# Row maxima rounded on VectorE, output weights loaded behind them, and four smaller moves of work in a fused transformer block

## The chip, the core and the metric

The kernel runs on one core of one Trainium2 chip. The time is device microseconds of one execution, from its start to its end. Three runs of the kernel before took 1684.24, 1685.24 and 1686.47 us; their median, 1685.24 us, is the figure that a change is compared with. A further execution was taken with the hardware profiler; every row below is from it.

## The reference

A transformer block over 2048 rows of 512 numbers, in float32: layer norm with a shift and a scale, attention with 32 heads of 16, an output projection, a gated residual, then a second layer norm and a feed-forward network of 1792 with a tanh GELU.

```python
def reference(A_x, A_wqkv, A_wo, B_x, B_w1, B_b1, B_w2, B_b2, c, w_mod):
    x = A_x
    mod = (_silu(c) @ w_mod).reshape(c.shape[0], 6, 1, -1)
    sa, ca, ga, sb, cb, gb = (mod[:, i] for i in range(6))
    h = _layernorm(x, axis=-1) * (1 + ca) + sa
    x = x + ga * _A_ref(h, A_wqkv, A_wo)
    h = _layernorm(x, axis=-1) * (1 + cb) + sb
    x = x + gb * _B_ref(h, B_w1, B_b1, B_w2, B_b2)
    return x
```

`_A_ref` forms q, k and v, takes the softmax of q·k/4 over all 2048 keys for each head, multiplies it with v and projects the result with `wo`. `_B_ref` is `gelu(x @ w1 + b1) @ w2 + b2`.

## The kernel before

**Precision.** Operands of most matmuls are split into a high part (rounded to the matmul's own format) and a low part (the rest), and three products of the parts are added. That is why so many small steps "cast, then subtract" stand in the program.

**Units and half-steps.** Attention is cut into 32 *units*: a block of 512 rows (four blocks, 0 to 3) times a group of four heads. A unit has 16 *half-steps*, one for each 128 keys; there are 512 half-steps in all, numbered through. In one half-step TensorE does four score matmuls (`e`, L685), whose exponentials ScalarE takes (L692); four more score matmuls for the row maxima of a unit that comes later (`mx`, L415), which VectorE reduces (L420); up to six matmuls of *background* work on each half of the rows (`bg`, L279: projections of q, k, v at first, then output projection and feed-forward of the block before); and at its end the eight value matmuls (`pv`, L720). A row of `pv` therefore marks the end of a half-step, and the distance of two such rows is its length. When no background work is at hand, the half-step runs without it.

**Row maxima.** A softmax needs the maximum of each row before its exponentials. The 64 `mx` matmuls of a unit are spread over 16 half-steps and run `LEAD` = 80 ahead, so that a unit's last one falls into the eleventh half-step of the unit before. Their results rotate through three PSUM banks (3, 4, 5): the fourth `mx` of a half-step writes the bank that the first `mx` of the same half-step had, and must wait until VectorE has reduced that one. Where a half-step has no background work, the third `mx` goes to the background's own bank 7 instead. When the 64th reduction of a unit is recorded, `max_rows` adds four operations: VectorE takes the minimum over the key blocks (L433, values are negated) and transposes it (L435); GpSimd rounds it (L437) and forms the rest (L438). SyncE stores both to DRAM (L442) three ticks later and loads them as two extra rows of the query tile `qst` (L448) six ticks later. The first `e` of the unit needs these rows. A *tick* is one `advance()`, one exponential; a half-step has four.

**Banks.** `e` has banks 0 to 2, `mx` 3 to 5, `pv` 6, the background 7. `take(name)` hands out the next bank of a ring.

**What else the change touches.** `turn_blocks` transposes blocks of v on VectorE (L345), at most two half-steps after the projection. `attn_out` copies the finished `pv` bank to SBUF at each unit's end (L707), on VectorE. `o_prep` loads a unit's denominators, takes reciprocals on VectorE (L767), spreads them over DRAM (L771, L777) and lets GpSimd divide (`div`, L787 to L789). `wload` asks for the next weights of the background (L835): `wo`, `w1`, `w2`. After the projections of block 0, `open_ffn` opens the pools of the feed-forward, four `wload` calls ask for `wo`, and the background pauses for `OPEN` ticks. `front` runs the output projection, the second layer norm (`stat`, `factor`, `norm`) and four groups of transposes (`trans`, L918), one group per half-step. `ffn1` takes the first feed-forward product: ScalarE (L948), GpSimd (L949 to L951), ScalarE's tanh (L954) in `second`, nine ticks later, and GpSimd again (L956 to L959).

The order on each engine is the order in which the program is written out, half-step by half-step (`half_step`); each engine takes its instructions strictly in that order. The line that decides which bank the third `mx` of a half-step without background takes is in `half_step`:

```python
fs.append(mx_mm(1 - a, "bg" if free and sum(xc) == nx - 2 else "mx"))
```

Of the kernel before, what the change touches and what calls it, by code (L numbers as in the profile page):

```python
# [61 lines left out]
RUN = 6  # L62
OPEN = 12
WB = 8
# [8 lines left out]
def block_kernel(ctx: ExitStack, tc: tile.TileContext, x, wqkv, wo, w1, b1, w2, b2, c, w_mod, out):  # L73
# [276 lines left out]
    def turn_blocks(hs):  # L350
        if not blocked:
            return
        if until_hs[0] is None:
            until_hs[0] = hs + 1
        left = until_hs[0] - hs
        n = len(blocked)
        rowed_now = rowed[0] >= clock["t"] - 4
        for _ in range(n if left <= 0 else 0 if rowed_now and n <= 2 * left else -(-n // (left + 1))):
            turn_block()
# [68 lines left out]
    rows, rowed = {}, [0]  # L428

    def max_rows(u):  # L430
        rowed[0] = clock["t"]
# [4 lines left out]
        m2 = small.tile([P, 2, 32], FR, tag="m2", name="m2")  # L436
        gp.tensor_copy(m2[:, 0], mt)  # L437
        gp.tensor_tensor(m2[:, 1], mt, m2[:, 0].bitcast(F32), op=ALU.subtract)  # L438

# [264 lines left out]
    def attn_out(u, pv):  # L704
        qb, g = divmod(u, NG)
        o = kqpool.tile([P, TB], F32, tag="osb", name="osb", bufs=1)
        saw(ve.tensor_copy(o, pv))  # L707
        rowed[0] = clock["t"]
        late = u < NU - 1
# [41 lines left out]

    free_pc, busy, over = [0], [0], [False]

    def o_prep(b, k):
# [30 lines left out]

        def div():
            eng.tensor_tensor(ob, ob, rb, op=ALU.mult)  # L787
            eng.tensor_copy(pc(b, k, 0), ob)
# [4 lines left out]
        fast = 0 < b < NB - 1 and k == KC - 1  # L793
        later(11 if over[0] else 28 if b == 0 and k < KC - 1 else 9 if fast else 14, inv)

# [17 lines left out]
    for b in range(NB):  # L813
# [4 lines left out]
        if b < NB - 1:  # L818
            stream += [(b + 1, "o", k) for k in range(KC)]
    wt, used, ringed, extra = {}, set(), [], []  # L820

    def wload():

        n = len(wt)
        if n == len(stream) or "f" not in pools:
            return
# [29 lines left out]
    def front(b, x2):  # L856
# [9 lines left out]
        def norm(t):  # L866
# [4 lines left out]
            if len(xn) == 4:  # L871
                later(5, lambda: sides.extend([lambda fc=fc: trans(fc, "mx") for fc in range(KC)]))

        def stat(t):
# [9 lines left out]
            def whole():  # L884
                ve.bn_aggr(mv[:, t], st)
                factor(t)

            def calm(f):
                later(3, f) if rowed[0] > clock["t"] - 4 else f()

# [38 lines left out]
    def feed(b, x2):  # L929
# [7 lines left out]
        def ffn1(i):  # L937
            def evac(ps):
# [22 lines left out]

                later(9, second)

# [41 lines left out]
    def block0():  # L1005
# [346 lines left out]
```

## Time and profile before

| what | us |
|---|---|
| median of three runs | 1685.24 |
| profiled execution, its own time | 1683.93 |
| its span, first to last instruction | 1682.1 |
| TensorE busy | 1656.0 |
| VectorE busy | 1424.9 |
| ScalarE busy | 1211.3 |
| GpSimd busy | 716.7 |
| mean granted TensorE clock, as a share of full speed | 0.993 |

The profiled execution is 1.3 us faster than the median of the three runs and 1.8 us longer than its own span. A row of the timeline gives the start and the duration in us, the engine (PE is TensorE, PEld its weight loads, DVE VectorE, ACT ScalarE, POOL GpSimd, SPq the queue of SyncE), the line, the operation, the tile written and the tiles read, and the count of like instructions merged into the row; in brackets stands the idle time ahead of it and what ended it. A row of the groups gives the count, then the busy time, the mean duration in ns, and the idle time ahead.

### The profile page before, as it was taken

The page shows a single profiled execution, that of the slowest core. Times are in us where ns is not written, and L with a number is a line of the kernel's source. Part 1 is how long each engine was busy: PE and PEld are TensorE (multiplying, and loading weights), DVE is VectorE, ACT ScalarE, POOL GpSimd, SP SyncE. Part 2 cuts the span into 40 slices and gives each one's busy share as a digit, 9 for nine tenths or more (in the row PEclk, how much of TensorE's full clock was granted, in tenths as well). Part 3 has the DMA queues.
Part 4 walks back from the last instruction along what each step waited for, and adds up shares of the span by engine and source line. Part 5 has one row for each costly group of instructions (what it writes and reads, how often), then busy time and mean ns, then how long its engine had stood idle before and what let it go on. Part 6 is the DMA issues. An engine that isn't in the chain of part 4 may idle for free.

```text
span 1682.1 us, 32274 instructions
## 1 busy us (share of the span) xinstructions
PE 1656.0 (98%) x12079; PEld 905.8 (54%) x12079; DVE 1424.9 (85%) x2770; ACT 1211.3 (72%) x2320; POOL 716.7 (43%) x719
## 2 busy tenths in 40 slices
PE   7999999999998999999999999999999999999999
PEld 6655555555544455555555555555555555553677
DVE  7999999999898999999999899999999899990332
ACT  4367777777776788778777888778777887788131
POOL 7443544534221376216523476126434475056210
PEclk8999999999999999999999999999999999999999
DMA  8766666665546443335462554254452643252544
GB/s 289 212 196 181 222 214 207 224 175 191 152 146 200 119 113 102 78 97 142 115 170 59 152 156 106 68 141 138 106 152 56 185 128 84 64 166 72 185 152 159
DMA packets 142808, 246.97 MB, mean 147 GB/s; under 512 B 25390, under 2 KB 53052, under 8 KB 142652
## 3 DMA queue, kind: packets, MB, share of 16 engines
q1 hardware_dynamic: 140896, 243.80, 49.8%
q8 instruction: 96, 1.57, 0.4%
q10 hardware_dynamic: 1756, 1.11, 0.3%
q14 instruction: 60, 0.49, 0.1%
HBM read 184.56 MB, written 60.29 MB: 146 GB/s over the span
## 4 chain that ended last, share of the span: by engine, by line
PE 93%; DMA 3%; DVE 2%; POOL 1%; ACT 0%; SPq 0%; issue 0%; POOLq 0%; ACTq 0%; DVEq 0%
PE bg L279 40%; PE pv L720 29%; PE e L685 16%; PE mx L415 4%; PE pr L279 2%; DMA wraw<-in_A_wqkv_dram 1%; DVE mxp L420 1%; PE o L279 1%; DMA qk<-parts 0%; DVE hTlo L510 0%; PE mx L918 0%; DMA m<-m 0%; DMA wt<-wos 0%; POOL wqkv L210 0%; DMA qst<-m 0%
## 5 line engine op out<-in xcount | busy, mean ns | idle before, releaser
L420 DVE TENSOR_REDUCE mxp<-mx 128x1 f32<-128x512 f32 x2038 | 1288.1, 682 | 116.7 <-PE mx L415 102.2
L692 ACT ACTIVATE p<-e 128x512 f32<-128x512 f32 x2048 | 1072.4, 608 | 307.9 <-PE mx L415 265.6
L415 PE MATMUL mx<-kh,qst 48*128 48x512 f32 x2038 | 842.2, 424 | 0.7 <-DVE mxp L420 0.5
L685 PE MATMUL e<-qst,kh 50*128 50x512 f32 x2048 | 777.3, 423 | 10.6 <-DMA qst<-m 5.3
L685 PEld LDWEIGHTS e<-qst,kh 50*128 50x128 f32 x2048 | 342.4, 185 | 440.6 <-ACT p L692 327.2
L720 PE MATMUL pv<-p,vg 128*17 128x512 f32 x4096 | 541.1, 599 | 0.1
L415 PEld LDWEIGHTS mx<-kh,qst 48*128 48x128 f32 x2038 | 369.8, 185 | 18.8 <-DVE mxp L420 9.4
L279 PE MATMUL bg<-w,g 64*128 64x512 f32 (+1 forms) x1080 | 269.7, 389 | 0.0
L279 PEld LDWEIGHTS bg<-w,g 64*128 64x128 f32 (+1 forms) x1080 | 200.4, 186 | 30.8 <-POOL g L958 0.9
L279 PE MATMUL bg<-pchi,w 64*128 64x512 f32 x672 | 182.9, 391 | 0.0
L720 PEld LDWEIGHTS pv<-p,vg 128*17 128x17 f32 x4096 | 68.2, 95 | 170.6 <-issue 168.8
L279 PE MATMUL bg<-hThi,wqkv 64*128 64x512 f32 x560 | 153.4, 393 | 0.0
L279 PEld LDWEIGHTS bg<-pchi,w 64*128 64x128 f32 x672 | 123.9, 185 | 23.0 <-DVE tick L1135 5.1
L279 PEld LDWEIGHTS bg<-hThi,wqkv 64*128 64x128 f32 x560 | 103.9, 186 | 12.4
L956 POOL TENSOR_SCALAR s<-s 128x512 f32<-128x512 f32 x42 | 62.9, 1497 | 82.5 <-ACT s L954 81.7
L279 PE MATMUL bg<-pclo,w 64*128 64x512 f32 x336 | 91.9, 392 | 0.0
L975 POOL TENSOR_TENSOR x<-y,x 128x512 f32<-128x512 f32 x28 | 36.0, 1286 | 125.5 <-ACT y L974 125.5
L279 PE MATMUL bg<-hTlo,wqkv 64*128 64x512 f32 x280 | 76.2, 391 | 0.0
L949 POOL TENSOR_TENSOR s<-h 128x512 f32<-128x512 f32 x42 | 43.8, 1042 | 74.9 <-ACT h L948 74.9
L279 PEld LDWEIGHTS bg<-pclo,w 64*128 64x128 f32 x336 | 61.7, 185 | 14.5 <-DVE tick L1135 3.4
L279 PE MATMUL bg<-wo,pchi 64*128 64x512 f32 x192 | 60.4, 395 | 0.0
L437 POOL CAST m<-mt 128x32 fp32r<-128x32 f32 x32 | 6.8, 212 | 123.1 <-DVE mt L435 123.1
(162 smaller groups left out, 1359.3 us busy)
## 6 DMA issues: line engine op xcount, KB each, us to landing
kh<-qk SPq DMA_DIRECT2D x256, 192.0 KB
w<-w2s SPq DMA_DIRECT2D x56, 512.0 KB
w<-w1s SPq DMA_DIRECT2D x54, 512.0 KB
qk<-parts SPq DMA_DIRECT2D x32, 512.0 KB
vg<-v SPq DMA_DIRECT2D x48, 272.0 KB
qst<-qk SPq DMA_DIRECT2D x64, 192.0 KB
qk<-parts SPq DMA_DIRECT2D x32, 256.0 KB
ou<-osb SPq DMA_DIRECT2D x32, 256.0 KB
```

The costliest lines, as they stand in the source:

```text
L279: return te.matmul(ps, term[0][r], rhs, start=i == 0, stop=i == n - 1)
L415: te.matmul(ps, qst[u][r0 : r0 + KR, p, qc * P : (qc + 1) * P], kh(u, kr // 2)[r0 : r0 + KR, p, (kr % 2) * TB : (kr % 2 + 1) * TB], start= ...
L420: ins = ve.tensor_reduce(mxp[u][:, hc, kr : kr + 1], ps, axis=AX.X, op=ALU.max, negate=True)
L437: gp.tensor_copy(m2[:, 0], mt)
L685: ins = te.matmul(ps, kh(u, kc // 8)[r0 : r0 + KX, p, (kc % 8) * P : (kc % 8 + 1) * P], qst[u][r0 : r0 + KX, p], start=True, stop=True)
L692: op = ac.activation(t, ps, AF.Exp, scale=SCALE)
L720: te.matmul(pvb[32 * j : 32 * j + VW], vg[u % 2][:, n : n + VW], pt.pop(4 * s + j), start=kc == 0, stop=kc == NKC - 1)
L949: gp.tensor_tensor(s, h, h, op=ALU.mult)
L956: gp.tensor_scalar(s, s, 1.0, None, op0=ALU.add)
L975: later(4, lambda: gp.tensor_tensor(x2[t], y, x2[t], op=ALU.add))
```

## The change

```diff
-OPEN = 12
+OPEN = 14
+WAIT = 6
...
 def turn_blocks(hs):
-        rowed_now = rowed[0] >= clock["t"] - 4
+        rowed_now = rowed[0] >= clock["t"] - 4 or hs and hs % NKC == 0
         for _ in range(n if left <= 0 else 0 if rowed_now and n <= 2 * left else -(-n // (left + 1))):
...
+    def calm(f):
+        if rowed[0] > clock["t"] - 4 or cur["pv"] % NKC == NKC - 1:
+            later(2, lambda: calm(f))
+        else:
+            f()
...
 def max_rows(u):
-        gp.tensor_copy(m2[:, 0], mt)
-        gp.tensor_tensor(m2[:, 1], mt, m2[:, 0].bitcast(F32), op=ALU.subtract)
+        ve.tensor_copy(m2[:, 0], mt)
+        ve.tensor_tensor(m2[:, 1], mt, m2[:, 0].bitcast(F32), op=ALU.subtract)
...
 def attn_out(u, pv):
-        saw(ve.tensor_copy(o, pv))
-        rowed[0] = clock["t"]
+        if act["g"]:
+            saw(ve.tensor_copy(o, pv))
+            rowed[0] = clock["t"]
+        else:
+            ac.activation(o, pv, AF.Copy)
...
 def div():
+            divided[0] = clock["t"]
...
-        later(11 if over[0] else 28 if b == 0 and k < KC - 1 else 9 if fast else 14, inv)
+        later(11 if over[0] else 28 if b == 0 and k < KC - 1 else 9 if fast else 14, inv if over[0] else lambda: calm(inv))
...
 def wload():
-        if n == len(stream) or "f" not in pools:
+        if n == len(stream) or "f" not in pools or not wready:
...
-                later(5, lambda: sides.extend([lambda fc=fc: trans(fc, "mx") for fc in range(KC)]))
+                later(5, lambda: sides.extend([lambda fc=fc: trans(fc, "mx" if b or fc == KC - 1 else "bg") for fc in range(KC)]))
...
 def stat(t):
-            def calm(f):
-                later(3, f) if rowed[0] > clock["t"] - 4 else f()
...
 def ffn1(i):
-                later(9, second)
+                t0 = clock["t"]
+                later(9, lambda: later(6, second) if divided[0] > t0 - 4 else second())
...
 def block0():
         open_ffn()
+        yield from wait(WAIT)
+        wready.append(True)
         for k in range(KC):
             wload()
-        yield from wait(OPEN)
+        yield from wait(OPEN - WAIT)
```

The lines move by up to eleven: L420, L433, L435 of the kernel before are L421, L440, L442 of the changed one; its new VectorE operations are L444 and L445.

**Place one, the end of block 0's projections** (half-steps 138 to 143, unit 8). On VectorE, the row maxima of unit 9 (`mn`, `mt`, `m`), between reductions (`mxp`) of `mx` banks. Before:

```order
L420 TENSOR_REDUCE mxp<-mx 128x1 x5
L433 TENSOR_REDUCE mn_181<-mxp 128x16
L435 STREAM_TRANSPOSE mt<-mn_181 128x32
L420 TENSOR_REDUCE mxp<-mx 128x1 x2
L420 TENSOR_REDUCE mxp<-bg 128x1
```

VectorE in the changed kernel, at the same place:

```order
L421 TENSOR_REDUCE mxp<-mx 128x1 x5
L440 TENSOR_REDUCE mn_181<-mxp 128x16
L442 STREAM_TRANSPOSE mt<-mn_181 128x32
L444 CAST m_7431<-mt 128x32
L445 TENSOR_TENSOR m_7431<-mt,m_7431 128x32
L421 TENSOR_REDUCE mxp<-mx 128x1 x2
L421 TENSOR_REDUCE mxp<-bg 128x1
```

The cast and the subtraction now stand on VectorE between the transpose and the next reduction; the same two rows are gone from GpSimd. This holds for all 32 units.

SyncE at the same place: stores of projected parts (`qk`), loads of `wo`, the store of the maxima (`m`), their load into `qst`, loads of keys (`kh`) and of the first feed-forward weights (`w1s`). Before:

```order
L302 DMA qk_86<-parts 128x512
L835 DMA wo<-wos_135 128x1024
L835 DMA wo<-wos_136 128x1024
L835 DMA wo<-wos_137 128x1024
L835 DMA wo<-wos_138 128x1024
L442 DMA m_104<-m_7431 4x32x32 x2
L835 DMA w_7498<-w1s_139 128x1024
L448 DMA qst<-m_104 2x1024 x2
L387 DMA kh_194<-qk_88 48x2x512 x2
```

SyncE in the changed kernel:

```order
L303 DMA qk_86<-parts 128x512
L449 DMA m_104<-m_7431 4x32x32 x2
L455 DMA qst<-m_104 2x1024 x2
L846 DMA wo<-wos_135 128x1024
L846 DMA wo<-wos_136 128x1024
L846 DMA wo<-wos_137 128x1024
L846 DMA wo<-wos_138 128x1024
L388 DMA kh_194<-qk_88 48x2x512 x2
L846 DMA w_7566<-w1s_139 128x1024
```

The maxima and their load stand ahead of the four `wo` loads, where they stood behind them and behind one `w1s` load. The background pauses in the same half-steps as before (139 to 142, and 159 to 164).

**Place two, TensorE at the transposes of block 0** (`ident,xn`), in a half-step without background. Before, from one `pv` to the next:

```order
L685 MATMUL e<-qst,kh_193 128x512
L415 MATMUL mx<-kh_195,qst 128x512
L685 MATMUL e<-qst,kh_193 128x512
L415 MATMUL mx<-kh_195,qst 128x512
L685 MATMUL e<-qst,kh_193 128x512
L415 MATMUL bg<-kh_195,qst 128x512
L685 MATMUL e<-qst,kh_193 128x512
L415 MATMUL mx<-kh_195,qst 128x512
L918 MATMUL mx<-ident,xn 128x128 x4
L720 MATMUL pv<-p,vg_1175 17x512 x4
```

TensorE in the changed kernel, the end of the first half-step with transposes:

```order
L692 MATMUL e<-qst,kh_193 128x512
L416 MATMUL bg<-kh_195,qst 128x512
L692 MATMUL e<-qst,kh_193 128x512
L416 MATMUL mx<-kh_195,qst 128x512
L926 MATMUL bg<-ident,xn 128x128 x4
L730 MATMUL pv<-p,vg_1175 17x512 x4
```

Three of the four groups now write bank 7 (`bg`), which the third `mx` of the same half-step has just written; each group also stands one half-step later (162 to 165 instead of 161 to 164), so that the fourth falls into a half-step with background.

**Place three, GpSimd in unit 30**: two divisions (`ob`, `kh`) of the last block, and two feed-forward pieces (`s`, `h`, `g`). Before:

```order
L787 TENSOR_TENSOR ob<-ob,rb 128x512
L788 CAST kh_197<-ob 128x512
L789 TENSOR_TENSOR kh_197<-ob,kh_197 128x512
L956 TENSOR_SCALAR s<-s 128x512
L957 TENSOR_TENSOR h<-s,h 128x512
L958 CAST g<-h 128x512
L959 TENSOR_TENSOR g<-h,g 128x512
L787 TENSOR_TENSOR ob<-ob,rb 128x512
L788 CAST kh_197<-ob 128x512
L789 TENSOR_TENSOR kh_197<-ob,kh_197 128x512
L949 TENSOR_TENSOR s<-h 128x512
L950 TENSOR_SCALAR s<-s 128x512
```

GpSimd in the changed kernel:

```order
L798 TENSOR_TENSOR ob<-ob,rb 128x512
L799 CAST kh_197<-ob 128x512
L800 TENSOR_TENSOR kh_197<-ob,kh_197 128x512
L798 TENSOR_TENSOR ob<-ob,rb 128x512
L799 CAST kh_197<-ob 128x512
L800 TENSOR_TENSOR kh_197<-ob,kh_197 128x512
L964 TENSOR_SCALAR s<-s 128x512
L965 TENSOR_TENSOR h<-s,h 128x512
L966 CAST g<-h 128x512
L967 TENSOR_TENSOR g<-h,g 128x512
L957 TENSOR_TENSOR s<-h 128x512
L958 TENSOR_SCALAR s<-s 128x512
```

The second part of the first piece moved behind the second division; both still stand ahead of the second piece. On ScalarE the tanh of the first piece moved from half-step 486 to 488; the tanh of the second piece stays at the end of half-step 490. In unit 31 one more tanh moved by two half-steps.

Elsewhere: two of the 32 copies of `pv` go to ScalarE (after half-step 159 and after the last one); two reciprocals stand after a unit's end instead of ahead of it (after half-step 255 and 383); some statistics move by one to three half-steps. The transposes of v stand in the same half-steps and the same order as before: `turn_blocks` meets four waiting blocks with one half-step left, and 4 <= 2·1 is false, whatever `rowed_now` is.

More of the change, by code (lines that the diff above doesn't have):

```diff
@@ L750, in tmp @@
         return dvpool.tile([P, D], F32, tag="t", name=name, bufs=4)
-    free_pc, busy, over = [0], [0], [False]
+    free_pc, busy, over, divided = [0], [0], [False], [-99]
     def o_prep(b, k):
@@ L819, in block_kernel @@
             stream += [(b + 1, "o", k) for k in range(KC)]
-    wt, used, ringed, extra = {}, set(), [], []
+    wt, used, ringed, extra, wready = {}, set(), [], [], []
     def wload():
         n = len(wt)
-        if n == len(stream) or "f" not in pools:
+        if n == len(stream) or "f" not in pools or not wready:
             return
```

## The prediction, as it was put on record

> **What bounds the kernel now.** I read the page first, then the list of waits, then TensorE's timeline from one `pv` to the next, and last the timelines of the engines that TensorE waits for.
>
> ```profile
> PE 1656.0 (98%) x12079; PEld 905.8 (54%) x12079; DVE 1424.9 (85%) x2770; ACT 1211.3 (72%) x2320; POOL 716.7 (43%) x719
> ```
>
> TensorE is busy 98% of the span of 1682.1 us. A saving off TensorE is therefore worth only the hole in TensorE's row that it closes, and a delay elsewhere costs whatever hole it opens. So I look for holes, half-step by half-step.
>
> ```profile
> 316.96 1.05 PE L720 MATMUL pv<-p,vg 128*17 128x512 f32 x8
> ...
> 317.95 0.49 PE L415 MATMUL mx<-kh,qst 48*128 48x512 f32 x1
> ...
> 319.46 0.40 PE L415 MATMUL mx<-kh,qst 48*128 48x512 f32 x1
> 319.79 1.05 PE L720 MATMUL pv<-p,vg 128*17 128x512 f32 x8
> ```
>
> This is an ordinary half-step: 319.79 - 316.96 = 2.83 us from `pv` to `pv`. The first `mx` stands at 317.95, the fourth at 319.46, 1.51 later. It is the one in which unit 5's maxima are finished, and VectorE does this in it:
>
> ```profile
> 318.19 0.22 DVE L433 TENSOR_REDUCE mn<-mxp 128x16 f32<-128x64 f32 x1
> 318.52 0.21 DVE L435 STREAM_TRANSPOSE mt<-mn 128x32 f32<-128x32 f32 x1
> 318.65 1.84 DVE L420 TENSOR_REDUCE mxp<-mx 128x1 f32<-128x512 f32 x3
> ```
>
> The two small operations push the reduction of the first `mx` to 318.65, 0.70 after that matmul's start, and TensorE does not notice. What happens when VectorE is pushed further is seen at unit 0's end, where the copy of `pv` and two transposes of v stand ahead of the reduction:
>
> ```profile
> 148.74 1.05 PE L720 MATMUL pv<-p,vg 128*17 128x512 f32 x8
> 149.73 0.49 PE L415 MATMUL mx<-kh,qst 48*128 48x512 f32 x1
> ...
> 151.65 0.50 PE L415 MATMUL mx<-kh,qst 48*128 48x512 f32 x1
> 152.08 1.05 PE L720 MATMUL pv<-p,vg 128*17 128x512 f32 x8
> ```
>
> ```profile
> 150.92 1.87 DVE L420 TENSOR_REDUCE mxp<-mx 128x1 f32<-128x512 f32 x3
> ```
>
> The first reduction starts 1.19 after its matmul; the fourth `mx`, which needs its bank, starts at 151.65 instead of 149.73 + 1.51 = 151.24, `pv` follows it by 0.43 instead of 0.33, and the half-step takes 3.34, 0.51 too long. So with d the distance from the first `mx` to its reduction, the loss is about d - 0.69 once d is over 0.7 (0.70: nothing; 1.19: 0.51). **VectorE has no room left in the half-step of the row maxima.**
>
> **Rounding on VectorE.** It adds a cast and a subtraction of 128x32 at exactly that place. No row shows them on VectorE; their neighbours are:
>
> ```profile
> L788 DVE CAST kh<-ob 128x512 fp32r<-128x512 f32 x1 | 0.4, 426 | 0.0
> L789 DVE TENSOR_TENSOR kh<-ob,kh 128x512 fp32r<-128x512 f32 x1 | 0.7, 693 | 0.0
> L223 DVE TENSOR_TENSOR s_c<-s_c,c_c 128x4 f32<-128x4 f32 x1 | 0.2, 163 | 0.0
> L196 DVE CAST hThi<-h 128x512 fp32r<-128x512 f32 x1 | 1.1, 1082 | 0.0
> ```
>
> Between 163 ns at 4 columns and 693 at 512, the subtraction of 32 columns takes about 0.19 us. The cast is 426 at 512; with a fixed part like the subtraction's it takes about 0.17. Each operation of this chain needs the result before it, and L435 starts 0.11 after L433's end (318.41 to 318.52), while the reduction starts 0.08 ahead of L435's end. So the reduction moves by 0.11 + 0.17 + 0.11 + 0.19 = 0.58; without any waiting between them, by 0.36. I take 0.50. Then d is 0.70 + 0.50 = 1.20 and the loss 0.51 per unit, with ends of 0.37 and 0.59. It falls on 29 units: of the 31 whose successors' maxima are finished inside the loop, unit 8 has no background there and so one `mx` less in the ring, and after unit 30's there is no reduction left. 29 x 0.51 = **+14.8 us** (10.7 to 17.1), and the first unit's maxima lie on a VectorE chain at the start, +0.4. Bounds further out: nothing, if the two overlapped entirely; and, by the cast that took 1082 ns where another took 426, 2.5 times the two durations, 0.36 x 1.5 = 0.54 more, 29 x 0.54 = 16 us on top.
>
> [...]
>
> **Maxima ahead of the output weights.** The one large hole in the steady part is in half-step 143:
>
> ```profile
> PE e L685 <- DMA qst<-m: 5.3, 2, 4.8
> ```
>
> ```profile
> 502.90 0.46 SPq L302 DMA_DIRECT2D qk<-parts  x1
> 506.37 1.75 SPq L835 DMA_DIRECT2D wo<-wos  x4
> ```
>
> ```profile
> 510.11 1.05 PE L720 MATMUL pv<-p,vg 128*17 128x512 f32 x8
> 515.99 0.76 PE L685 MATMUL e<-qst,kh 50*128 50x512 f32 x1 [4.83 <-DMA qst<-m]
> ...
> 519.42 1.58 PE L720 MATMUL pv<-p,vg 128*17 128x512 f32 x8
> ```
>
> The half-step takes 519.42 - 510.11 = 9.31, 6.48 too long. The store of the maxima stood behind four `wo` loads on SyncE, which themselves waited until 506.37, and its data behind their 2 MB. TensorE stood still for 4.83 and then ran slowly (0.76 for an `e` that otherwise takes 0.49), which the next half-step also feels, by some 0.5. In the changed order the store goes out right after 503.36, the load follows before 507.5, and `e` finds its rows at 511.1. **-6.5 - 0.5 = -7.0.** What is late next is `wo`.
>
> ```profile
> 514.32 0.57 SPq L448 DMA_DIRECT2D qst<-m  x2
> ```
>
> It is asked for about 1 us later than before, near 507.4, and its first quarter is needed at 511.4; before, all four quarters and the maxima had landed by 514.32, when SyncE could go on to the load, 7.9 after the first issue. A quarter of that is 2.0, so the first should be there near 509.5 to 510.5, the second a little before its use at 512.1. I take no wait; the far end is a wait of 2 us, +2. SyncE's other issues (keys, `x`, values) move behind by the same microsecond and stand some 5 us earlier in absolute time. The second, 0.5 us wait of the two above is on maxima that GpSimd rounded late: -0.5.
>
> **Transposes in bank 7.** Before:
>
> ```profile
> 568.06 1.05 PE L720 MATMUL pv<-p,vg 128*17 128x512 f32 x8
> ...
> 572.22 1.05 PE L720 MATMUL pv<-p,vg 128*17 128x512 f32 x8
> ...
> 574.81 0.65 PE L918 MATMUL mx<-ident,xn 128*128 128x128 f32 x4
> 575.40 1.05 PE L720 MATMUL pv<-p,vg 128*17 128x512 f32 x8
> ```
>
> ```profile
> 574.98 0.68 DVE L420 TENSOR_REDUCE mxp<-bg 128x1 f32<-128x512 f32 x1
> ```
>
> The transposes start at 574.81, while VectorE reads bank 7 until 575.66. Writing that same bank they must wait for it: 0.85 to 0.9 us in each of three half-steps, +2.6; these become about 4.05 long instead of 3.18. The shift by a half-step takes the first group out of half-step 161 (4.16 long, with VectorE behind), -1.2, leaves VectorE's backlog to the next, +0.3, and puts the last group, 0.59, into a full half-step, +0.6. ScalarE's copy of `pv` there spares VectorE 0.6 at a place with slack. Sum **+2.3** (from -1, if the bank's wait were hidden, to +3.5).
>
> **The tanh.** In half-step 490 ScalarE waits in front of the second tanh:
>
> ```profile
> 1511.45 1.30 POOL L787 TENSOR_TENSOR ob<-ob,rb 128x512 f32<-128x512 f32 x1
> ...
> 1516.58 1.26 POOL L951 TENSOR_TENSOR s<-s,h 128x512 f32<-128x512 f32 x1
> ```
>
> ```profile
> 1517.88 0.63 ACT L954 ACTIVATE s<-s 128x512 f32<-128x512 f32 x1 [3.77 <-POOL s L951]
> ```
>
> GpSimd worked without a gap from 1511.45 to 1517.84, and ScalarE, with all exponentials behind that tanh, stood for 3.77. The change delays the first piece's tanh and lets the second division go ahead of its rest; but division, rest and the second piece's three operations all stay ahead of the second tanh, in another order. The same work ends no earlier, and later by whatever the second division waits for its data. I take +0.6 for that and for one tanh more in a half-step where ScalarE already has an extra evacuation (from -3.8, the whole stall, to +1.5).
>
> **The rest.**
>
> ```profile
> 841.31 0.34 DVE L767 RECIPROCAL dn<-dn 128x32 f32<-128x32 f32 x1
> ```
>
> This reciprocal, and one like it in unit 23, stood between the last reduction and the copy at a unit's end; moved out, each gives back at most its 0.34, together -0.5 with rounding up. The three ends of units 0, 2 and 4 with transposes of v, 0.5 each, stay: the order shows the transposes unmoved. The pause of 14 ticks for 12 costs nothing, since the background rests in the same half-steps; the last copy on ScalarE is as long as VectorE's.
>
> **Sum:** 14.8 + 0.4 - 7.0 - 0.5 + 2.3 + 0.6 - 0.5 = +10.1. Against the profiled execution's own 1683.9 that is 1694.0; the median of the runs shown lies 1.3 above that execution, so I put it at **1695**.
>
> **The rivals.**
>
> *The rounding is hidden* (the other side: faster). It decides at d: if the reduction still starts within 0.7 of its matmul, TensorE never waits and 14.8 goes: 1695 - 15 = 1680. For it speaks that VectorE is busy only 85% and idles later in each half-step; against it, that 0.70 is used already and that unit 0's end shows the loss at 1.19. The two operations would have to cost 0.02 together, less than a tenth of the smallest row. 8%.
>
> *The rounding is stretched* by GpSimd at work beside it, as the cast of 1082 ns was: +16, half of it more likely than all, so 1703 to 1711. For it: GpSimd is busy 43% of the span. Against: the two operations have 32 columns, and their fixed part need not stretch. 9%.
>
> *The wait moves from the maxima to `wo`*: TensorE stands at 511.4 for up to 2 us, and if it then runs slowly as it did after 515.99, for one more: 1697 to 1699. For it: the loads are asked for later and needed at the same time. Against: 4 us lie between. 10%.
>
> *The tanh or the transposes gain after all*, as a change that reorders them may mean to: -3 to -4 each at best, 1688 to 1692. Against: the orders, in which the same work stays ahead. 10%.
>
> *The change doesn't do what it says*: for the V blocks this is certain, and already in the sum at 0.
>
> **How the numbers follow.** My forecast has 63%, by its own bounds (10.7 to 17.1 for the rounding, +2 for `wo`, -3 and +1 for the transposes) 1689 to 1701. With the two rivals next to it the range must reach down to 1686 and up to 1702; outside lie the hidden rounding and most of the stretched one, some 17%. A measurement of this kernel can tell about 0.2% from no change, 3.4 us. Faster than 1681.9: 8% from the hidden rounding and 1% from several small gains together. Between 1681.9 and 1688.6: 11%, a rounding of half the price or two gains at once. Slower: 80%.
>
> **What would show it.** In the changed kernel's timeline, half-steps 16u + 11 should be 3.2 to 3.45 long with the cast and subtraction of some 0.17 and 0.19 on VectorE and d near 1.2; at 2.85 the rounding is hidden. Half-step 143 should be near 2.85 without a wait on `qst`; a wait there on `wo` is the third rival. Half-steps 162 to 164 should be near 4.05, with TensorE waiting on VectorE's `bg` reduction. The tanh in half-step 490 should still wait for L959 (L951 before) by nearly 4 us. I am wrong if the `mx` ring has slack that I don't see, or if VectorE's small operations overlap more than L433 and L435 do.

## The result, and the profile after

| | before | after |
|---|---|---|
| median, us | 1685.86 (4 runs, 1684.24 to 1686.54) | 1712.07 (4 runs, 1706.44 to 1712.49) |
| profiled execution, its own time, us | 1683.93 | 1711.76 |
| its span, us | 1682.1 | 1709.9 |
| first `pv`, last `pv`, at us | 106.3, 1561.6 | 106.6, 1589.3 |

The ratio is 1.0149, with a 95% interval from 1.0127 to 1.0172: the change made the kernel **slower by 1.5%**, 26 us, where 10 were forecast. The first row of the changed kernel's page (busy time of each engine):

```profile
PE 1669.8 (98%) x12079; PEld 905.9 (53%) x12079; DVE 1446.6 (85%) x2832; ACT 1212.7 (71%) x2322; POOL 702.9 (41%) x655
```

TensorE is busy for 13.8 us more with the same 12079 instructions, and the span is 27.8 longer. Where the rest went is found as the prediction looked for holes: all 511 intervals from one `pv` to the next are measured in both traces and subtracted, pair by pair (counted from 0, so that interval 142 is half-step 143, and the eleventh interval of unit u is half-step 16u + 11). Outside the places named here the pairs agree within some 0.04 us. Three of the places differ between profiles even where nothing was changed at them, so one pair of traces does not decide them: the start, the second wait on `qst` and the half-steps behind the tanh. They are taken up below.

| place | forecast, us | measured, us |
|---|---|---|
| row maxima: 29 eleventh half-steps, 23.1; the one behind unit 3's, 1.55; the one behind unit 8's, 0.67 | +14.8 | +25.3 |
| start, up to the first `pv` | +0.4 | +0.3 |
| maxima ahead of `wo` (half-steps 143, 144) | -7.0 | -6.5 |
| second wait on `qst` | -0.5 | -0.6 |
| rows of `x` for block 0 (half-steps 149 to 151) | 0 | +3.4 |
| transposes of block 0 | +2.3 | +3.0 |
| tanh: the half-step of the second piece's, and the four around it | +0.6 | +2.7 |
| reciprocals (0.2 each); statistics moved (0.15 at three places) | -0.5 | 0.0 |
| transposes of v | 0 | 0 |
| **sum** | **+10.1** | **+27.6** |

**The row maxima.** TensorE and then VectorE in unit 13 of the changed kernel, where GpSimd rests (start and duration in us):

```profile
750.76 1.05 PE L730 MATMUL pv<-p,vg 128*17 128x512 f32 x8
...
751.75 0.49 PE L416 MATMUL mx<-kh,qst 48*128 48x512 f32 x1
...
754.06 1.05 PE L730 MATMUL pv<-p,vg 128*17 128x512 f32 x8
```

```profile
752.07 0.22 DVE L440 TENSOR_REDUCE mn<-mxp 128x16 f32<-128x64 f32 x1
752.32 0.21 DVE L442 STREAM_TRANSPOSE mt<-mn 128x32 f32<-128x32 f32 x1
752.57 0.18 DVE L444 CAST m<-mt 128x32 fp32r<-128x32 f32 x1
752.78 0.19 DVE L445 TENSOR_TENSOR m<-mt,m 128x32 fp32r<-128x32 f32 x1
752.89 1.88 DVE L421 TENSOR_REDUCE mxp<-mx 128x1 f32<-128x512 f32 x3
```

With the first `mx` at 751.75, d is 1.14 and d - 0.69 = 0.45; the interval is 3.30, which is 0.47 over the ordinary 2.83 and 0.40 over the same half-step before (2.90). The forecast was 0.51. Now unit 4, VectorE first, then GpSimd, then TensorE at the same moment:

```profile
326.59 0.21 DVE L442 STREAM_TRANSPOSE mt<-mn 128x32 f32<-128x32 f32 x1
326.84 1.09 DVE L444 CAST m<-mt 128x32 fp32r<-128x32 f32 x1
327.96 0.53 DVE L445 TENSOR_TENSOR m<-mt,m 128x32 fp32r<-128x32 f32 x1
328.41 1.87 DVE L421 TENSOR_REDUCE mxp<-mx 128x1 f32<-128x512 f32 x3
```

```profile
326.61 1.28 POOL L316 TENSOR_TENSOR parts<-pf,parts 128x512 fp32r<-128x512 f32 x1
327.83 0.62 POOL L660 CAST wsp<-wf 128x512 fp32r<-128x512 f32 x1
```

```profile
326.08 0.49 PE L416 MATMUL mx<-kh,qst 48*128 48x512 f32 x1
...
329.14 0.50 PE L416 MATMUL mx<-kh,qst 48*128 48x512 f32 x1 [1.15 <-DVE mxp L421]
```

The cast ends at 327.93, 0.04 after GpSimd's subtraction (327.89). The next VectorE instruction ends at 328.49, 0.04 after GpSimd's cast (328.45). The small instructions are not slowed by some factor: they **stand until GpSimd's running instruction has ended**. Then d is 328.41 - 326.08 = 2.33, d - 0.69 is 1.64, and the interval was 1.65 too long: the formula held, d did not. I call this the *hold*. Over the kernel it shows in the means, which lie well above the 0.18 and 0.19 of unit 13 (groups, 32 instructions each):

```profile
L444 DVE CAST m<-mt 128x32 fp32r<-128x32 f32 x32 | 14.5, 453 | 1.1
...
L445 DVE TENSOR_TENSOR m<-mt,m 128x32 fp32r<-128x32 f32 x32 | 9.6, 301 | 1.1
...
L442 DVE STREAM_TRANSPOSE mt<-mn 128x32 f32<-128x32 f32 x32 | 6.8, 212 | 1.1
```

The transpose keeps 212. The loss is 1.2 to 2.3 us in seven of the units 0 to 7, where GpSimd prepares weights, and 1.1 in units 15 and 23, where it divides. It is 0.63 in units 9, 12, 20 and 28, where the cast is held for some 0.24, and 0.38 to 0.49 in the rest of the 29.

**Maxima ahead of `wo`, and what came behind.** SyncE's queue in the changed kernel:

```profile
516.43 1.57 SPq L449 DMA_DIRECT2D m<-m  x2
519.92 0.57 SPq L455 DMA_DIRECT2D qst<-m  x2
520.67 1.76 SPq L846 DMA_DIRECT2D wo<-wos  x4
...
528.97 0.34 SPq L720 DMA_DIRECT2D ou<-osb  x1
529.72 0.57 SPq L639 DMA_DIRECT2D vg<-v  x1
530.55 4.01 SPq L865 DMA_DIRECT2D x<-in_A_x_dram  x4
```

Half-step 143 fell from 9.31 to 3.31 us, with no wait on `qst` or `wo`. But the rows of `x` are now asked for behind the copy of `pv` and the values, and their issue alone takes 4.01. Before, they stood ahead of both:

```profile
517.66 3.29 SPq L854 DMA_DIRECT2D x<-in_A_x_dram  x4
...
522.47 0.33 SPq L710 DMA_DIRECT2D ou<-osb  x1
```

GpSimd and then VectorE in the changed kernel:

```profile
543.23 1.28 POOL L915 TENSOR_TENSOR x<-y,x 128x512 f32<-128x512 f32 x1 [27.75 <-DMA qst<-qk]
```

```profile
544.54 0.43 DVE L893 BATCH_NORM_STATS2 bsh<-x 128x6 f32<-128x256 f32 x1 [1.92 <-POOL x L915]
544.89 1.87 DVE L421 TENSOR_REDUCE mxp<-mx 128x1 f32<-128x512 f32 x3
```

The same instruction in the kernel before:

```profile
529.37 1.29 POOL L907 TENSOR_TENSOR x<-y,x 128x512 f32<-128x512 f32 x1 [26.43 <-ACT y L904]
```

ScalarE's copy of the first output group, which that instruction adds to `x`, before and after:

```profile
528.68 0.62 ACT L904 ACTIVATE y<-bg 128x512 f32<-128x512 f32 x1
```

```profile
535.82 0.62 ACT L912 ACTIVATE y<-bg 128x512 f32<-128x512 f32 x1
```

Before, the addition started 0.07 behind the copy's end; now it starts at 543.23, 6.8 behind it, and waits for a transfer. The profile names `qst` as what ended the wait, the neighbour of `x` on the queue; that it was `x` is shown by the experiment that asks for `x` sooner. VectorE waits with the statistics of `x`, the reductions that the program puts behind them wait too, and TensorE loses 3.4 in three half-steps.

**Transposes and tanh.** TensorE at the second group of transposes, and ScalarE at the tanh of the second piece:

```profile
590.55 0.66 PE L926 MATMUL bg<-ident,xn 128*128 128x128 f32 x4 [0.83 <-DVE mxp L421]
591.14 1.05 PE L730 MATMUL pv<-p,vg 128*17 128x512 f32 x8
```

```profile
1545.09 0.63 ACT L962 ACTIVATE s<-s 128x512 f32<-128x512 f32 x1 [5.75 <-POOL s L959]
```

The groups wait for the reduction of bank 7 as forecast; half-steps 162 to 164 take 4.41, 4.08 and 4.08. The tanh waits 5.75 where it waited 3.77. GpSimd shows why:

```profile
1530.31 1.28 POOL L800 TENSOR_TENSOR kh<-ob,kh 128x512 fp32r<-128x512 f32 x1
1533.67 1.29 POOL L798 TENSOR_TENSOR ob<-ob,rb 128x512 f32<-128x512 f32 x1 [2.08 <-DMA w<-w2s]
```

The second division now follows the first directly, its data are not there, and GpSimd stands idle for 2.08 us; before, the rest of the first piece filled that time. Not all of the +2.7 is this. Behind the stall TensorE's granted clock is 0.5 for 6.8 us (1544.1 to 1551.0), where in the profile of before it was 0.5 for 3.4 (1520.6 to 1524.1). So the next half-step is 0.99 longer, and it is just as much longer in seven profiles of kernels below whose tanh stands as before, with a slow clock as long as here. How much the tanh cost by itself is shown by undoing it.

### The profile page after: what moved, and what is told of

It is laid out like the page before. It is cut to its first block, busy times and chain, and to the rows that moved or that the text cites. A ratio compares the mean times of both kernels' runs of the same rounds, so it can differ in the third digit from the quotient of the medians.

```text
span 1709.9 us, 32270 instructions
## 1 busy us (share of the span) xinstructions
PE 1669.8 (98%) x12079; PEld 905.9 (53%) x12079; DVE 1446.6 (85%) x2832; ACT 1212.7 (71%) x2322; POOL 702.9 (41%) x655
## 4 chain that ended last, share of the span: by engine, by line
PE 84%; DVE 8%; DMA 4%; POOL 1%; issue 1%; SPq 1%; ACT 1%; POOLq 0%; ACTq 0%; DVEq 0%
PE bg L280 35%; PE pv L730 27%; PE e L692 15%; DVE mxp L421 5%; PE mx L416 5%; PE pr L280 1%; DMA rden<-dn 1%; DMA x<-in_A_x_dram 1%; DMA kh<-qk 1%; DVE m L444 1%; DVE bst L238 1%; DMA wm<-in_w_mod_dram 0%; PE o L280 0%; DVE m L445 0%; PE mx L926 0%
## 5 line engine op out<-in xcount | busy, mean ns | idle before, releaser
L421 DVE TENSOR_REDUCE mxp<-mx 128x1 f32<-128x512 f32 x2038 | 1288.6, 682 | 118.5 <-PE mx L416 101.9
L964 POOL TENSOR_SCALAR s<-s 128x512 f32<-128x512 f32 x42 | 62.9, 1498 | 112.5 <-ACT s L962 112.5
L280 PEld LDWEIGHTS bg<-pclo,w 64*128 64x128 f32 x336 | 61.7, 185 | 13.8 <-DVE tick L1146 4.3
L315 POOL CAST parts<-pf 128x512 fp32r<-128x512 f32 x23 | 14.1, 612 | 119.4 <-ACT pf L314 119.4
```

What stands on the lines that cost most here:

```text
L280: return te.matmul(ps, term[0][r], rhs, start=i == 0, stop=i == n - 1)
L315: gp.tensor_copy(parts[:, 0], r)
L421: ins = ve.tensor_reduce(mxp[u][:, hc, kr : kr + 1], ps, axis=AX.X, op=ALU.max, negate=True)
L964: gp.tensor_scalar(s, s, 1.0, None, op0=ALU.add)
```

## The experiments

A single profiled time is uncertain by its start: the first `pv` came between 104.3 and 108.2 us in the twelve profiles of this study, though at most two small instructions on one unit's maxima differ there. So the intervals decide, most of which repeat to some 0.02. The profile of before has one of its own: the second wait on `qst`, 0.47 in interval 110, is 0.12 in one other profile and missing in ten, also where GpSimd rounds as before. So the -0.6 there cannot be put down to the change.

### Undo the rounding; do it alone

The first kernel is the changed one with this edit; the second makes the opposite edit in the kernel before, and no other.

```diff
-        ve.tensor_copy(m2[:, 0], mt)
-        ve.tensor_tensor(m2[:, 1], mt, m2[:, 0].bitcast(F32), op=ALU.subtract)
+        gp.tensor_copy(m2[:, 0], mt)
+        gp.tensor_tensor(m2[:, 1], mt, m2[:, 0].bitcast(F32), op=ALU.subtract)
```

> The changed kernel with only the rounding of the maxima put back on GpSimd. The theory (the hold: VectorE's cast and subtraction within SBUF stand still until the GpSimd instruction that runs beside them has ended, so the rounding cost 23.1 us in the eleventh intervals of 29 units, 1.5 in the interval behind unit 3's and 0.7 behind unit 8's) says the profiled execution falls by about 25 us, from 1711.8 to 1686 or 1687, with no eleventh interval over 2.9 us. The rival (the rounding cost the 14.8 us of the prediction, and 10 us come from other parts of the change) says 1696 to 1698, with some of the long intervals left. Either way the 3.4 us at the block 0 input rows (three intervals from 148 on), the 3.0 at the transposes and the 2.7 at the tanh should stay, and the interval 142 should stay near 3.3 if the maxima ahead of the output weights are enough, or rise towards 3.8 if VectorE's quicker rounding was needed as well.

> The kernel before with nothing but the rounding of the maxima on VectorE. The hold says +25 us: 1709, with the eleventh intervals of units 0 to 7 at 1.2 to 2.3 over the ordinary 2.83 where GpSimd's TENSOR_TENSOR or CAST of the weights' preparation runs beside the cast, 0.4 to 0.5 where GpSimd rests or runs a TENSOR_SCALAR, and 1.1 to 1.2 in units 15 and 23, where it divides. The prediction's fixed price says +15: 1699, 0.51 in each of 29 units. GpSimd's program loses 64 short instructions, so the places at which it is beside the cast can move by some tenths of a us.

Measured: 1683.09 with the rounding put back, the eleventh intervals of units 0 to 29 equal to those of before within 0.03. Alone it gave 1710.07, beside 1684.93 for the kernel before on the same chip: +25.1; the intervals at the maxima sum to +24.6. So **the rounding is the whole loss**; the other parts of the change together are worth about nothing (by intervals -6.5 in half-steps 143 and 144, +1.6 at `x`, +3.0 at the transposes and +2.7 at the tanh, the latter in part the slow clock). Half-step 143 stayed at 3.33: the order on SyncE is enough there, VectorE's quicker rounding (0.18 and 0.19 us in unit 13, where GpSimd's two took 0.21 and 0.25 on average) adds nothing. In the kernel with the rounding alone unit 3 cost 2.55 + 2.28 + 0.51; the last two come with a granted TensorE clock of 0.5 from 279.2 to 286.0 us. Unit 0 lost 0.40 instead of 1.88 and unit 5 0.46 instead of 1.38: where GpSimd happens to be decides.

### The same place, instructions that are not held

```diff
         ve.transpose(mt, m)
+        ve.transpose(m, mt)
+        ve.transpose(mt, m)
```

> The kernel before with two more transposes of 128x32 behind L435 (the maxima turned back and turned again, some 0.21 us each), the rounding still on GpSimd. They stand on VectorE at the very place of the changed kernel's cast and subtraction and are about as long, but read one SBUF tile each, as the transpose that is there and is never stretched. The hold says that they cost the fixed price alone in every unit, 0.45 to 0.55 in units 0 to 7 as in the others, and 29 x 0.5 = 14.5: 1698. The rival, that whatever stands at this place of VectorE is stretched by the load of the first eight units (their memory traffic, or TensorE's), says 1.2 to 2.3 in units 0 to 7 again, and 1707 to 1709.

Measured: 1696.55, and in every unit from 0 to 29 but 8 an interval 0.42 to 0.51 longer, most 0.48, the first eight like the others. Together +13.9: the forecast's 14.8 was right for the fixed price. What is left, 25.3 - 13.9 = **11.4 us**, is the hold with the slow half-steps behind it. The split is good to about 1 us: the units of the changed kernel in which nothing is held lost 0.38 to 0.49, a little less than the transposes cost.

### A GpSimd instruction set beside the cast

```diff
         ve.tensor_reduce(m[:, :16], mxp.pop(u), axis=AX.X, op=ALU.min)
+        if u > 10:
+            d = ga_b.rearrange("p (a b) -> p a b", b=32)
+            s = m[:, None, :].to_broadcast([P, 16, 32])
+            if u % 3 == 0:
+                gp.tensor_tensor(d, s, d, op=ALU.add)
+            elif u % 3 == 1:
+                gp.tensor_scalar(d, s, 1.0, None, op0=ALU.add)
+            else:
+                gp.tensor_copy(d, s)
```

> The kernel before with the rounding of the maxima on VectorE, and beside it, for the maxima of units 11 to 31, one extra GpSimd instruction of 128x512 that starts once L434 has the maxima: a TENSOR_TENSOR (1.3 us) where the unit's number is divisible by 3, a TENSOR_SCALAR (up to 1.5 us) where it leaves 1, a COPY (0.6 us) where it leaves 2. What it writes is used by nobody. If the hold is real and belongs to the instruction, the eleventh interval of the unit before grows from 0.4 to 0.5 over 2.83 to about 1.2 to 1.6 beside the TENSOR_TENSOR (the cast takes 0.9 to 1.1 us), stays at 0.4 to 0.6 beside the TENSOR_SCALAR (cast under 0.25), and goes to 0.6 to 0.9 beside the COPY (cast 0.4 to 0.5): about 6 us in all over the kernel with the rounding alone. If the long casts of units 0 to 7 came from what those units load and store, and not from GpSimd's instruction, all three kinds leave the interval at 0.4 to 0.6.

Three units of this kernel, each VectorE's cast and GpSimd's instruction beside it:

```profile
661.70 1.13 DVE L446 CAST m<-mt 128x32 fp32r<-128x32 f32 x1
```

```profile
661.50 1.29 POOL L438 TENSOR_TENSOR ga_b<-mn,ga_b 128x512 f32<-128x512 f32 x1 [3.24 <-DVE mn L433]
```

```profile
708.51 0.45 DVE L446 CAST m<-mt 128x32 fp32r<-128x32 f32 x1
```

```profile
708.32 1.49 POOL L440 TENSOR_SCALAR ga_b<-mn 128x512 f32<-128x512 f32 x1 [6.67 <-DVE mn L433]
```

```profile
754.71 0.50 DVE L446 CAST m<-mt 128x32 fp32r<-128x32 f32 x1
```

```profile
754.56 0.61 POOL L442 COPY ga_b<-mn 128x512 f32<-128x512 f32 x1 [10.93 <-DVE mn L433]
```

Beside TENSOR_TENSOR and COPY the cast ends 0.04 after GpSimd's instruction, as expected, and the intervals are 1.4 and 0.7 longer than before (2.7 and 1.75 where a second GpSimd instruction catches the subtraction as well). Beside the TENSOR_SCALAR I was wrong: the cast takes 0.45, not under 0.25, and the intervals are 0.73 to 0.83 longer. The cast ends at 708.96, 0.64 after the TENSOR_SCALAR's start, and so does the cast beside each other TENSOR_SCALAR within 0.01; the last 0.85 us of that GpSimd record hold nobody. That also explains why the changed kernel's casts beside L964, a TENSOR_SCALAR that had started 0.45 earlier, took 0.19: 0.64 - 0.45. The kernel took 1726.56, some 16 more than with the rounding alone. I had expected about 6; the intervals of units 10 to 29 gave 12, and the slow half-steps behind units 23 and 28 another 3. I had left out the units in which two instructions are caught, and what they bring behind them.

### Which VectorE instructions are held

The kernel before, with GpSimd's TENSOR_TENSOR as above in units 11 to 31 and one spare instruction of 128x32 on VectorE, in four forms by turns (cast, `tensor_scalar`, `tensor_tensor`, copy).

> The kernel before, the rounding on GpSimd as it was, with a GpSimd TENSOR_TENSOR of 128x512 (1.3 us) that starts once the maxima are there (units 11 to 31), and behind L437 on VectorE one extra instruction of 128x32 whose result nobody uses: a cast where the unit's number is divisible by 4, a TENSOR_SCALAR where it leaves 1, a TENSOR_TENSOR where it leaves 2, a plain COPY where it leaves 3. The hold as read so far says that cast and TENSOR_TENSOR stand until GpSimd's instruction has ended (0.8 to 1.1 us instead of 0.2). For TENSOR_SCALAR and COPY there is no row so far: if every VectorE instruction that writes SBUF from SBUF waited, they would too, though the transpose of the same size never has; I expect the COPY to wait like the cast and leave the TENSOR_SCALAR open. L434 and L437 themselves should keep 0.22 and 0.21.

Groups of VectorE's instructions in this kernel (count, busy us, mean ns, idle time before):

```profile
L433 DVE TENSOR_REDUCE mn<-mxp 128x16 f32<-128x64 f32 x32 | 7.0, 220 | 2.2
...
L438 DVE STREAM_TRANSPOSE mt<-mn 128x32 f32<-128x32 f32 x32 | 6.8, 212 | 2.7
...
L448 DVE COPY gb_b<-mt 128x32 f32<-128x32 f32 x6 | 6.3, 1044 | 0.2
...
L446 DVE TENSOR_TENSOR gb_b<-mt,mn 128x32 f32<-128x32 f32 x5 | 5.5, 1100 | 0.2
...
L442 DVE CAST gb_b<-mt 128x32 fp32r<-128x32 f32 x5 | 5.4, 1072 | 0.2
L444 DVE TENSOR_SCALAR gb_b<-mt 128x32 f32<-128x32 f32 x5 | 5.3, 1057 | 0.2
```

All four forms take 1.04 to 1.10 us on average (the spare COPY of unit 31's maxima stands beside another instruction), and each ends 0.04 to 0.06 behind GpSimd's instruction. The transpose keeps its 212 although it overlaps the same GpSimd instruction; the reduction has ended when that one starts, so it is not tested here. The held instruction cost 1.16 to 1.21 in each of 20 units: 1710.14 in all, beside 1686.31 for the kernel before.

So the wait ends with GpSimd's instruction: 0.04 to 0.06 us behind it in this kernel, some 0.04 in the changed one. Beside GpSimd's TENSOR_SCALAR it ended earlier, 0.64 us into the 1.49 that the trace gives it. What in the chip makes VectorE wait, no run shows.

### A later place for the rounding

The kernel before with the rounding on VectorE, but given out 4 or 8 ticks later, store and load of the maxima with it.

```diff
+        later(4 if u else 0, round_rows)
...
-            later(3, store)
-            later(6, load)
+            later(7, store)
+            later(10, load)
```

> The kernel before with the rounding on VectorE, but 4 ticks later: behind the second reduction after the maxima instead of ahead of the first (store and load of the maxima 4 ticks later too). In an ordinary half-step the first reduction starts 0.57 behind its matmul, where 0.69 is free, and VectorE idles 0.3 us. If the fixed price of 0.48 in every unit comes from the place, ahead of the reduction that frees the first bank, the eleventh interval is ordinary again, the next one loses 0.0 to 0.3, and units 9 to 29 together lose at most 6 us instead of 10. If it comes from VectorE's work as such, the 0.48 stays in the one or the other. Where GpSimd runs a TENSOR_TENSOR beside it (units 0 to 7, 15, 23) the hold stays, and 0.3 to 1.5 are lost in the twelfth interval. Sum: 1690 to 1697 if place decides, 1708 if not. The store of unit 9's maxima falls behind one more transfer: interval 142 up to 2 us longer.

> The same with the rounding 8 ticks later: one half-step further on, behind the second reduction there, when VectorE has caught up. If place decides, the twelfth and thirteenth intervals of quiet units are ordinary to 0.05, and only the hold of units with a GpSimd instruction beside the cast is left, lessened by the slack: 2 to 8 us in all, 1688 to 1694. If VectorE's work as such decides, 1708 again.

Measured: 1706.64 and 1705.07, beside 1686.22. The mechanism was right: in units where GpSimd rests, as 12, 20, 24 and 29, neither the eleventh nor any later interval differs from before by more than 0.08, in either kernel. Three more such units, 9, 17 and 25, lose 0.18 to 0.27 in the twelfth interval in the first kernel, within the 0.0 to 0.3 that was expected. So most of the fixed price of 0.48 **is the place**, ahead of the reduction that frees the first bank. The totals were wrong, for two reasons that the expectation lacked. At the new place other GpSimd instructions stand beside it: in the first of the two kernels eight of the units 10 to 29 run into a TENSOR_TENSOR and lose 0.93 to 0.98 in the twelfth interval. And the maxima now reach `qst` too late for some units. These are the first two of TensorE's waits in the first kernel (total, times, longest); the second line is background matmuls that wait for the held VectorE:

```profile
PE e L688 <- DMA qst<-m: 12.2, 5, 6.5
PE bg L279 <- DVE tick L1160: 8.0, 11, 1.2
```

### The output weights alone, `x` sooner

Of the change only `WAIT`, `OPEN` and the order of the weights, in the kernel before, and

```diff
-        later(9, lambda: load_x2(b, x2))
+        later(9 if b else 2, lambda: load_x2(b, x2))
```

> The kernel before with only the output weights asked for behind the maxima (WAIT 6 and OPEN 14 as in the change), and the input rows of block 0 asked for 7 ticks sooner, so that they stand ahead of the copy of pv, the values and one pair of w1 loads on SyncE, where they stood in the kernel before too. If the wait of 3.4 us in three intervals from 148 on comes from the place of these rows on SyncE, it is gone and 6.5 or more remain of the gain: 1677. If it comes from the volume (some 7 MB are due between the maxima and the first output projection, in 6 us less than before), the rows land no sooner, or the values behind them land late: 1679 to 1681, with a wait of 2 to 4 us there or at the next unit's start.

Measured: 1675.22 beside 1684.93. Half-steps 143 and 144 gave 6.4, and half-steps 149 to 151 were those of before within 0.01. So the late `x` was a matter of when SyncE asks for it, not of the volume. The gain of this part is the 6.4; the total is lower by more because the first `pv` came 1.8 earlier than in the profile of before and the wait in interval 110 was not there.

### Bank and tanh undone

The changed kernel with the rounding back on GpSimd, all four groups of transposes in the `mx` ring, and `later(9, second)` as before.

> The changed kernel with the rounding back on GpSimd, the transposes of block 0 back in the mx ring, and the tanh without its wait for a division. Against the kernel with only the rounding put back (1683.1): the transposes should give 3.0 us (three half-steps from 4.08 to 3.19) and the tanh 2.0 to 2.6 (its wait from 5.8 back to about 4), so 1677.5 to 1678. If the bank and the tanh were not the cause, and the half-steps there are long for want of the values they transpose or because GpSimd is behind for another reason, 1682 to 1683. The 1.6 us at the input rows of block 0 (interval 148) should stay.

Measured: 1679.9 beside 1683.09, on another chip. By intervals the transposes gave back 3.0 (half-steps 162 to 164: 3.21, 3.19, 3.19) and the tanh 1.9 (its wait 3.66 us instead of 4.92). Both causes stand. The other 0.8 of the tanh's 2.7 stayed, with a slow clock that is 6.8 us long here too. The total gave 3.2 only, because this execution reached its first `pv` 2.6 later and lost 1.1 in one half-step of unit 18, which no other profile shows and whose cause stays open. The wait for `x` was 0.6 here and 1.6 with the rounding alone put back, in programs that are the same up to there: it varies from run to run.

### Each part where it pays

> What is left of the change when each part is kept only where it pays: output weights behind the maxima, with the input rows of block 0 asked for 7 ticks sooner (1675.2 alone); reciprocals out of the units' ends (-0.4); rounding on GpSimd; transposes in the mx ring; the wait of the tanh given to the second piece instead of the first (six ticks more, so that GpSimd has its L962 done: the wait of 4 us and the slow clock behind it go, -3 to -4); and the transposes of v really moved out of the unit's end, by one half-step when four blocks wait there (three ends, 0.5 each: -1.2 to -1.5, if the half-steps behind take two transposes each without loss). Sum 1675.2 - 0.4 - 3.5 - 1.3 = 1670, a ratio of 0.991. If the tanh's wait moves to the next piece, 1673.

The edits beside those above, in the changed kernel:

```diff
+        if rowed_now and hs and hs % NKC == 0 and left == 1 and n == 4:
+            until_hs[0] += 1
+            return
...
-                later(9, lambda: later(6, second) if divided[0] > t0 - 4 else second())
+                later(15 if b == NB - 2 and divided[0] > clock["t"] - 12 else 9, second)
```

Measured in 4 runs: 1670.57 (1669.53 to 1673.86) beside 1686.31 (7 runs, 1683.91 to 1688.53), a ratio of 0.9912, interval 0.9894 to 0.9930: **faster than both kernels**, and 0.9% faster than the one before. The forecast of 1670 was met, in part by chance: it started from 1675.2, a time with an early first `pv`, and the half-steps at the tanh gave over 4 us where 3.5 was put. The waits of TensorE (total, times, longest) no longer show a single one over 1.6 us in their first lines, and VectorE copies `pv` with no transpose of v in front:

```profile
PE e L695 <- ACT p L702: 2.3, 10, 0.3
PE pr L507 <- DVE parts L544: 1.9, 2, 1.6
```

```profile
148.51 0.68 DVE L718 COPY osb<-pv 128x512 f32<-128x512 f32 x1
149.11 1.87 DVE L424 TENSOR_REDUCE mxp<-mx 128x1 f32<-128x512 f32 x3
...
151.57 0.49 DVE L346 STREAM_TRANSPOSE vst<-vr 128x128 f32<-128x128 f32 x2
```

The three ends of units with transposes of v took 2.95 instead of 3.34, -0.4 each; the half-step of the second tanh took 2.65 instead of 6.12, since it no longer waits. TensorE's granted clock is 1.0 from 41 to 1666 us in this kernel; the slow stretches behind the two stalls are gone with them.

## Why the prediction was wrong

The direction was right and the size was not: +26 against +10, outside the range that ended at 1702. Step by step:

- **Rounding on VectorE, "+14.8 (10.7 to 17.1)": the step that failed.** The half of it that was worked from rows held: d was 1.14 against 1.20, and the fixed price 13.9 against 14.8, as the two transposes show. The further bound was mis-sized. It made a stretch of 2.5 from one row, a cast of 1082 beside one of 426, put the whole at 16 and thought half of it likelier, and kept it out of the sum because "their fixed part need not stretch". The runs showed a wait in its place, whose length was what was left of GpSimd's TENSOR_TENSOR or CAST (the longest cast took 1.22 us and the longest subtraction 1.20, where alone they take 0.18 and 0.19); two such waits can follow each other, as in unit 3 (1.10 and 1.20). 11.4 us came on top. GpSimd's share of 43% was the wrong number to judge by. What counts is which GpSimd instruction runs in the eleventh half-step of each unit. The trace of before could have told a part of that: a TENSOR_TENSOR of GpSimd runs on for 1.0 to 1.4 us behind the transpose in units 1, 3, 4, 7 and 8, which all had a hold, and in unit 2, which had none. In most other units GpSimd's own rounding stood there, and what would run in its place had to be worked out.
- The rival "the rounding is stretched", 1703 to 1711, came nearest and had only 9%. The measured 1712.07 lies just past its end, and it had the wrong mechanism: a factor on VectorE's own time where the runs show a wait. The factor rested on one cast of 1082 ns, 128x512 and at 20.98 to 22.06 us of the trace of before, beside which GpSimd had a CAST from 20.73 to 21.77. That its price comes near is in part luck.
- **SyncE "(keys, `x`, values) … stand some 5 us earlier in absolute time": this failed too.** Counted from the `pv` that opens half-step 143 (510.11 and 523.80), the keys are 6.1 us earlier, but `x`, now behind two more transfers, is only 0.8 earlier (issued at 517.66 before, 530.55 after), while ScalarE's first copy of the output projection is 6.6 earlier. The forecast for `x` was 0; it cost 3.4, and 0.6 to 1.6 where the rounding was back on GpSimd.
- The maxima ahead of `wo` were right: -7.0 forecast, -6.5 measured, with no wait on `wo`.
- The transposes in bank 7 were right in mechanism and length (near 4.05, measured 4.41, 4.08, 4.08), +2.3 against +3.0, as undoing the bank shows.
- The tanh's cause was named (what the second division waits for its data) but priced at 0.6 together with one more tanh; the idle time is 2.08, and undoing the change gave 1.9. The rest of the +2.7 is slow clock that the profile of before happened to have for half as long.
- The second wait on `qst` (-0.5, measured -0.6) came out by luck: the prediction took it for a lasting cost of rounding on GpSimd, and it is gone or nearly gone in all other profiles, also where GpSimd rounds. The start (+0.4, measured +0.3) says nothing either, since the first `pv` moves by up to 4 us from one profile to the next.
- The reciprocals (0.2 each) were right; moved statistics gave their 0.4 back. The transposes of v did not move, as read from the order; moved for good they are worth 0.4 each.

## What to carry to other kernels

Before a copy, cast or elementwise instruction within SBUF is moved from GpSimd to VectorE, list what GpSimd will run at that moment: here the rest of a TENSOR_TENSOR or CAST of GpSimd came on top of VectorE's own time (1.09 us for a cast of unit 4 that takes 0.18 alone), and in nine units it cost more than that time. VectorE, 85% busy here, had no room at one place of its loop (0.48 lost) and room enough a half-step later (within 0.08 in four units where GpSimd rested), so measure the slack there, not the share. And when a stall is removed, whatever loaded its data during the stall may be late next, as `x` was here (3.4 us): move those loads with it.

## What the runs showed of the hardware

- A VectorE cast or TENSOR_TENSOR of 128x32 within SBUF stood until some 0.04 us after the end of a GpSimd TENSOR_TENSOR or CAST that had started first (up to 1.22 us in the changed kernel). The cast did so beside a GpSimd COPY too (0.50 us), and a VectorE copy and TENSOR_SCALAR beside a TENSOR_TENSOR (1.04 and 1.06 on average). Alone, the cast takes 0.18 and the TENSOR_TENSOR 0.19; the other two have no row alone. In unit 5 the cast started first (374.27, GpSimd's TENSOR_TENSOR at 374.34) and kept 0.18, and the subtraction behind it took 1.19. VectorE's transpose of 128x32 within SBUF kept 0.21 us in unit 4 (from 326.59) beside a TENSOR_TENSOR (326.61 to 327.89), and the reduction of 128x64 there kept 0.22 (326.34 to 326.56) beside a GpSimd CAST (325.91 to 326.52).
- GpSimd's TENSOR_SCALAR of 128x512, 1.49 us long in the trace, held VectorE only for its first 0.64 us.
- Behind a stall of 1.83 us in unit 3 of the changed kernel TensorE's `e` took 0.79 and 0.62 instead of 0.50 and 0.39, and the next half-step 4.39: 1.55 lost behind the 2.30 of the stall itself. The granted clock was 0.5 there for 3.4 us (281.2 to 284.6). The length of the stall alone does not decide it: in the kernel with a GpSimd instruction beside the cast, stalls of 1.86 (unit 3) and 2.31 (unit 20) had no slow clock behind them, and stalls of 1.27 (unit 0) and 1.31 (unit 28) had. What decides stays open.
